# Nine register loads for two, ScalarE scaling B rows in the prologue, and a later conversion of the capacity

## The chip, the cores and the metric

The kernel runs on one core of a Trainium2 chip. The metric is the device time of one execution in microseconds (us); lower is better. One core has five engines that run their own instruction streams in order and wait for each other on semaphores: TensorE (PE, with its weight loads shown apart as PEld), VectorE (DVE), ScalarE (ACT), GpSimd (POOL) and SyncE (SP, which here issues transfers).

## The reference, cut to what matters

Three parts follow one another: a linear attention with a decaying state, an MLP with h·cos(h), and a top-1 mixture of experts.

```python
# attention, chunk by chunk, for each of 4 x 8 heads (768 tokens, head_dim 32, d_state 16)
L = np.exp(cum[..., :, None] - cum[..., None, :]) * causal
y_intra = np.einsum('bhij,bhjd->bhid', np.einsum('bhin,bhjn->bhij', Cc, Bc) * L, xc)
y_inter = np.einsum('bhin,bhnd->bhid', Cc, state) * np.exp(cum)[..., None]
state = decay_full * state + np.sum(Bc * xc * np.exp(cum[..., -1:] - cum), axis=j)
# MLP over 3072 tokens of 256: w_in 256x2048, w_out 2048x256
h = x @ w_in;  x = (h * np.cos(h)) @ w_out
# experts: 8 of them, 256 -> 1024 -> 256, at most `capacity` tokens each
e = argmax(x @ w_gate);  keep the first `capacity` tokens of each expert
out[i] = gate_w[i] * (np.maximum(x[i] @ w1[e], 0) @ w2[e])   # kept tokens only
```

## The kernel before, in words

**Order of the work.** Each piece of work is a Python function that issues its instructions on whatever engines it uses. Pieces are registered with `put(name, fn, args)`; the n-th call for a name takes the n-th slot number of `PLACE[name]`, and at the end all pieces are run sorted by slot (L1739 on). That one order, written out by hand as a table of numbers, is the program order on every engine at once. A prologue that is listed in Python runs ahead of it.

**Attention** (first 300 us or so, mixed with the MLP). Tokens are cut into 24 chunks of 128, two chunks c = 0, 1 to a group g, so 12 groups. For group 1 in the prologue: `a_bcp` broadcasts the running sum of log a into PSUM (`bcp`, L700), `a_expp` turns it on ScalarE into the decay matrix `ex` (L708), `a_mask0` zeroes its upper triangle on GpSimd (L713; all columns but the last), `a_sd` makes the scores `spd` on TensorE (L732), which VectorE multiplies into `ex` (`a_md`, L740). `a_bp` (L676) scales the B rows of a chunk (`xb`, 128 tokens x 8 heads x 16) by the last column of that decay matrix, one factor per token and head; `a_up` and `a_st` (L766, L780 to L784) then build the state, `a_y` (L801, L806) the output, which is turned into `xT` (L845 on ScalarE, L851 on VectorE). The scores of chunk 1 of group 1 go into the PSUM banks in which its `bcp` stood.

**MLP.** Six tiles of 512 tokens. For each of 16 steps: `hp` (L921), on ScalarE and VectorE g = h·cos(h) (L928, L932, L935, L938), then `yt` (L959, L964). Its weights arrive as `pre` or `wst` and are split into a high and a low part by VectorE integer operations (L873, L878, L883).

**Experts.** Tokens are sorted into 29 to 31 blocks of 128 of one expert each, gathered by indirect transfer (L1535, `xr`) and transposed by DMA (L1552, `xkeep`, `xk`). A block has two halves of the hidden layer, so there are 58 jobs: `b_mm1` (L1603, `hp`), ReLU and its low part (L1609 ACT, L1613 DVE, `hr`), the transpose (L1630 `tp` on TensorE, copied by ACT L1639, or by DMA later), `b_mm2` (L1650, `yp`), the scaled sum (L1662, L1664, `yacc`) and the indirect write (L1669). The weights `w1a`, `w1b`, `w2a`, `w2b` of all 8 experts lie in SBUF, and a job picks its expert's by a register of TensorE's sequencer: `w[:, bass.ds(ev[i], 1)]`. The expert numbers of the blocks are worked out on VectorE into `eblk[0]` (blocks 0 to 11) and `eblk[1]` (19 entries from block 12 on; L1143), and `experts(k)` (L1589 to L1594) loads all of one of them with one `reg_load`. The second halves of the weights are still being normed while the first jobs run: `wst` is loaded (L1223), ScalarE sums squares (L1231), TensorE adds these up over partitions (L1235, `pn`), VectorE and others scale (L1240 to L1256).

**Capacity.** It comes as an int64, and `constants2` (slot 100) ends with four tiny VectorE operations that turn it into a float (L456 to L459, `capf`); its first reader is far behind, in the routing of the first tile.

Of the kernel before, what the change touches and what calls it, by code (L numbers as in the profile page):

```python
# [106 lines left out]
    'ete': [1446],
    'ets': [1431],
    'ett': [1438],
    'ex': [67, 116, 114, 159, 115, 240, 203, 390, 476, 493, 590, 597, 603, 738, 769, 849, 816,  # L110
        954, 870, 1082],
# [10 lines left out]
    'gat': [148, 230, 350, 466, 585, 713, 838, 944, 1049, 1185],  # L122
    'id': [1513],
    'in0': [1502],
    'in1': [1667],
    'iv0': [1499],
    'iv1': [1756, 1757, 1762],
    'lt': [1592],
    'lte': [1643],
    'lts': [1607],  # L130
    'ltt': [1623],
# [1680 lines left out]
```

## Time and profile before

| what | value |
| --- | --- |
| median of 3 runs | 568.72 us (568.5 to 569.3) |
| the profiled execution: its own time | 568.56 us |
| the profiled execution: its span | 566.8 us |
| TensorE (PE) busy | 528.7 us, 93% of the span |
| VectorE, ScalarE, GpSimd busy | 73%, 67%, 63% |
| chain that ended last, by engine | PE 45%, DVE 25%, ACT 11%, DMA 7%, issue 6% |
| granted TensorE clock, mean | 0.984 |

The span is counted from the first to the last instruction of the profile; the execution's own time is 1.8 us longer. Busy shares are means over stages with different limits: the first 80 us lean on VectorE and ScalarE, the rest for the most part on TensorE. "issue" is idle time for which the profile has no releaser. A timeline row has the start, the time from there to the end of a group of like instructions, and in brackets how long the engine sat idle before it and for whom.

### The profile page before, as it was taken

The numbers are of one execution on the slowest core, as the hardware profiler recorded it, in microseconds if no ns is written. First come the engines' busy times: TensorE is split into PE (matmuls) and PEld (weight loads), VectorE is DVE, ScalarE is ACT, GpSimd is POOL, SyncE is SP. The second block draws the span as 40 slices with busy tenths as digits, with TensorE's granted clock in tenths as the row PEclk, the third lists the DMA queues.
The fourth block names the chain that finished last, engine by engine and source line by source line (L and its number), as shares of the span: only waits on it lengthen the run. The fifth ranks groups of instructions, "written<-read, shape, count | busy, mean of one in ns | idle before, by whom it ended". The sixth has DMA issues, their size and how long they took to land.

```text
span 566.8 us, 10500 instructions
## 1 busy us (share of the span) xinstructions
PE 528.7 (93%) x3188; PEld 387.9 (68%) x3188; DVE 415.7 (73%) x877; ACT 379.2 (67%) x691; POOL 355.6 (63%) x422
## 2 busy tenths in 40 slices
PE   8778999999999999999999998899589999998993
PEld 7455666877878778887888686665357666665672
DVE  6999985669977987688788999989957632332441
ACT  5448998887788688868887887788388633323210
POOL 5775374878668869876955673887546454312454
PEclk9999999999999999999999998999789999999998
DMA  6898533666264365263522331576587688767882
GB/s 227 276 318 323 191 116 128 186 246 220 94 222 132 99 201 177 82 201 116 166 58 76 85 102 38 144 185 174 139 198 204 113 160 162 157 118 131 152 164 63
DMA packets 110645, 89.91 MB, mean 159 GB/s; under 512 B 64542, under 2 KB 99424, under 8 KB 110592
## 3 DMA queue, kind: packets, MB, share of 16 engines
q1 hardware_dynamic: 107808, 82.26, 52.5%
q0 software_dynamic: 2784, 6.97, 4.8%
q8 instruction: 30, 0.49, 0.4%
q14 instruction: 23, 0.19, 0.1%
HBM read 59.50 MB, written 15.54 MB: 132 GB/s over the span
## 4 chain that ended last, share of the span: by engine, by line
PE 45%; DVE 25%; ACT 11%; DMA 7%; issue 6%; POOL 3%; SPq 1%; POOLq 0%; ACTq 0%; DVEq 0%
PE hp L1603 10%; PE hp L921 9%; PE yp L1650 9%; PE yt L959 7%; DVE g L938 4%; DVE g L932 3%; ACT g L935 3%; DMA out_dram<-yacc,scat 2%; PE yt L964 2%; ACT ex L646 2%; ACT g L928 2%; DVE w2a L1256 1%; DVE xs L1037 1%; POOL out_dram L1669 1%; ACT gh L942 1%
## 5 line engine op out<-in xcount | busy, mean ns | idle before, releaser
L921 PE MATMUL hp<-xT,w_in 128*128 128x512 f32 x576 | 153.7, 406 | 4.7 <-DVE g L938 2.5
L921 PEld LDWEIGHTS hp<-xT,w_in 128*128 128x128 f32 x576 | 104.9, 189 | 35.0 <-DVE g L938 8.8
L947 POOL TENSOR_TENSOR gw<-g,gh 128x512 fp32r<-128x512 f32 x72 | 98.8, 1376 | 47.6 <-ACT gh L942 22.8
L959 PE MATMUL yt<-gh,w_o 128*128 128x512 f32 x320 | 88.4, 398 | 0.1
L935 ACT ACTIVATE g<-g,halfpi 128x512 f32<-128x512 f32 x96 | 67.9, 717 | 27.0 <-DVE g L932 26.4
L1650 PEld LDWEIGHTS <-ht 128*128 128x128 f16 x696 | 68.0, 98 | 20.7 <-issue 2.7
L1609 ACT ACTIVATE hr<-hp 128x512 f16<-128x512 f32 x58 | 33.7, 596 | 72.2 <-PE hp L1603 43.1
L938 DVE TENSOR_TENSOR g<-hp,g 128x512 f32<-128x512 f32 x96 | 65.4, 685 | 18.0 <-ACT g L935 17.8
L932 DVE SCALAR_TENSOR_TENSOR g<-g,hp 128x512 f32<-128x512 f32 x96 | 64.4, 679 | 16.9 <-ACT g L928 16.2
L1613 DVE SCALAR_TENSOR_TENSOR hr<-hp,hr 128x512 f16<-128x512 f32 x58 | 39.2, 686 | 40.0 <-ACT hr L1609 35.6
L959 PEld LDWEIGHTS yt<-gh,w_o 128*128 128x128 f32 x320 | 58.3, 188 | 12.7 <-issue 1.0
L928 ACT ACTIVATE g<-hp 128x512 f32<-128x512 f32 x96 | 55.0, 586 | 17.9 <-PE hp L921 15.3
L942 ACT ACTIVATE gh<-g 128x512 fp32r<-128x512 f32 x80 | 48.7, 622 | 11.0 <-DVE g L938 6.5
L959 PE MATMUL yt<-gw,w_o 128*128 128x512 f32 x160 | 50.9, 399 | 1.6 <-POOL gw L947 0.8
L1535 POOL DMA_INDIRECT xr<-xs_d,gat x29 | 34.3, 1181 | 20.0 <-DMA xk<-xr 7.5
L1650 PE MATMUL yp<-w2b,ht 128*128 x348 | 43.2, 272 | 1.7 <-ACT yacc L1662 1.6
L1650 PE MATMUL yp<-w2a,ht 128*128 x348 | 44.2, 274 | 0.4 <-ACT ht L1639 0.4
L1669 POOL DMA_INDIRECT out_dram<-yacc,scat x29 | 28.9, 997 | 23.1 <-DVE yacc L1664 15.7
L629 POOL TENSOR_TENSOR ex<-ex,ncum 128x512 f32<-128x512 f32 x32 | 37.5, 1193 | 3.3 <-DMA ex<-cumc_d 2.1
L1657 POOL TENSOR_TENSOR sc<-gall,invb 128x1 f32<-128x1 f32 x58 | 12.7, 231 | 42.2 <-ACT yacc L1662 30.9
L1664 DVE SCALAR_TENSOR_TENSOR yacc<-yp,sc,yacc 128x256 f32<-128x256 f32 x29 | 13.5, 481 | 32.3 <-PE yp L1650 23.6
L959 PEld LDWEIGHTS yt<-gw,w_o 128*128 128x128 f32 x160 | 29.5, 189 | 11.1 <-POOL gw L947 3.3
(244 smaller groups left out, 995.3 us busy)
## 6 DMA issues: line engine op xcount, KB each, us to landing
wst<-in_w_dram SPq DMA_DIRECT2D x32, 512.0 KB
ex<-cumc_d SPq DMA_DIRECT2D x10, 1024.0 KB
pre<-in_w_io_dram SPq DMA_DIRECT2D x14, 512.0 KB
hl_d<-hl SPq DMA_DIRECT2D x10, 512.0 KB
b<-hl_d SPq DMA_DIRECT2D x10, 512.0 KB
c4s<-hl_d SPq DMA_DIRECT2D x40, 128.0 KB
xb<-in_xB_dram SPq DMA_DIRECT2D x11, 384.0 KB
xs_d<-xs SPq DMA_DIRECT2D x6, 514.0 KB
```

Of the source, the lines that this page charges most:

```text
L629: nc.gpsimd.tensor_tensor(lt, lt, nn, op=ALU.add)
L921: nc.tensor.matmul(hp, w_in[:, f, wl, k, :], xT[:, k, xl, :], start=(n == 0), stop=(n == 5))
L928: nc.scalar.activation(g, HP[it], AF.Copy, bias=MAGIC + 0.25)
L932: nc.vector.scalar_tensor_tensor(g, g, MAGIC, HP[it], op0=ALU.subtract, op1=ALU.subtract)
L935: nc.scalar.activation(GT[it], GT[it], AF.Sin, scale=SIN_SCALE, bias=halfpi)
L938: nc.vector.tensor_tensor(GT[it], HP.pop(it), GT[it], op=ALU.mult)
L942: nc.scalar.activation(h, GT[it], AF.Copy)
L947: eng.tensor_tensor(l, GT.pop(it), GH[it][0].bitcast(F32), op=ALU.subtract)
L959: nc.tensor.matmul(YT[t][k], WO['w'][:, f, o, k * P:(k + 1) * P], r, start=(f == 0 and n == 0), stop=(f == NF - 1 and n == 2))
L1603: nc.tensor.matmul(hp, XK[i][:, 2 * xl + k, :], w[:, bass.ds(ev[i], 1), k, wl, :].rearrange("p a b -> p (a b)"), start=(n == 0), stop=(n = ...
L1613: nc.vector.scalar_tensor_tensor(hr[:, 1], HPB.pop(j), 0.0, hr[:, 0], op0=ALU.max, op1=ALU.subtract)
L1650: nc.tensor.matmul(yp, ht[:, hk, :], w[:, bass.ds(e, 1), k, wl, :].rearrange("p a b -> p (a b)"), start=(k == 0 and n == 0), stop=(k == 3 ...
```

## The change

Three edits, and a renumbering of the table that carries them.

First, `experts` loads a range of blocks and is called nine times, for 3, 3, 3, 3 registers of `eblk[0]` and 3, 3, 4, 4, 5 of `eblk[1]`; the same 31 registers in all. Second, the scaling of group 1's B rows, two VectorE operations in the prologue, becomes 16 ScalarE activations with a per-partition scale, 8 for each chunk. Third, the four capacity operations leave `constants2` and become a piece `cap` at slot 236. The rest of the table is only renumbered: apart from these pieces each engine has the order of before, and the orders of GpSimd and SyncE are the same throughout.

```diff
 PLACE = {
+    'cap': [236],
-    'ex0': [1472],
-    'ex1': [1658],
...
+    def cap_float():
         ci = cap_i.bitcast(I32)
         t = mp.tile([P, 4], F32, name="capt")
         nc.vector.tensor_copy(t[:, 0:2], ci)
...
+    def a_bpa(g, c):
+
+        d = G[g]
+        d['bp'] = d['btok']
+        bp = d['btok'][:, c, :].rearrange("p (v n u) -> p v n u", v=2, u=4)
+        for h in range(H):
+            x = bp[:, h // 4, :, h % 4]
+            nc.scalar.activation(x, x, AF.Copy, scale=d['lt'][c][:, h, P - 1:P])
...
-        (a_bp, 1, 0, V),
+        (a_bpa, 1, 0),
...
-        (a_bp, 1, 1, V),
+        (a_bpa, 1, 1),
...
-    def experts(k):
-        lo, hi = LOS[k]
-        regs = [nc.tensor.alloc_register(f"e{i}") for i in range(lo, hi)]
-        nc.tensor.reg_load(regs, eblk[k][0:1, 0:hi - lo])
-        for i, r in zip(range(lo, hi), regs):
+    def experts(k, a, b):
+        regs = [nc.tensor.alloc_register(f"e{i}") for i in range(a, b)]
+        nc.tensor.reg_load(regs, eblk[k][0:1, a - LOS[k][0]:b - LOS[k][0]])
+        for i, r in zip(range(a, b), regs):
             ev[i] = nc.tensor.snap(r, min_val=0, max_val=E - 1)
...
-    put('ex0', experts, 0)
+    for a, b in ((0, 3), (3, 6), (6, 9), (9, NE)):
+        put(f'e{a}', experts, 0, a, b)
...
-    put('ex1', experts, 1)
+    for a, b in ((12, 15), (15, 18), (18, 22), (22, 26), (26, LOS[1][1])):
+        put(f'e{a}', experts, 1, a, b)
```

On TensorE the second load of before (19 registers) stands between a job's `yp` and the next job's `hp`; the rows are those of before, where ISA is a register operation of the sequencer.

```order
L1650 LDWEIGHTS ht
L1650 ISA
L1650 MATMUL yp_4562<-w2a,ht 128x256
L1603 LDWEIGHTS xkeep_4156
L1592 TENSOR_LOAD eblk_90
L1594 ISA x2
L1603 ISA
L1603 MATMUL hp_4621<-w1a,xkeep_4156 128x512
```

In the changed kernel the same place has no load:

```order
L1668 LDWEIGHTS ht
L1668 ISA
L1668 MATMUL yp_4579<-w2a,ht 128x256
L1621 LDWEIGHTS xkeep_4166
L1621 ISA
L1621 MATMUL hp_4599<-w1a,xkeep_4166 128x512
```

One of the five that stand for it, the load of 4 registers for blocks 22 to 25, comes 930 rows further on, again between two `hp`:

```order
L1621 ISA
L1621 MATMUL hp_5189<-w1b,xk 128x512
L1621 LDWEIGHTS xk
L1610 TENSOR_LOAD eblk_90
L1612 ISA
L1621 MATMUL hp_5208<-w1a,xk 128x512
```

So one long load has become five short ones, each just ahead of the first job that needs it. On ScalarE in the prologue, before (`bcp_234` and `bcp_233` are the two PSUM banks of group 1's chunk 1):

```order
L651 ACTIVATE ex<-ex 128x256
L708 ACTIVATE ex<-bcp_234,ncum 128x128 x4
L892 ACTIVATE w_in<-w1a 128x256
L708 ACTIVATE ex<-bcp_233,ncum 128x128 x4
L845 ACTIVATE xT<-yp 128x2x128 x2
```

and in the changed kernel:

```order
L660 ACTIVATE ex<-ex 128x256
L696 ACTIVATE xb<-xb,ex 128x16 x8
L726 ACTIVATE ex<-bcp_234,ncum 128x128 x4
L910 ACTIVATE w_in<-w1a 128x256
L726 ACTIVATE ex<-bcp_233,ncum 128x128 x4
L696 ACTIVATE xb<-xb,ex 128x16 x8
L863 ACTIVATE xT<-yp 128x2x128 x2
```

The first eight scalings have moved in ahead of the two banks' exponentials, the second eight behind them. On VectorE the four capacity operations, in the changed kernel, stand between a weight split and the h·cos(h) step that followed it before:

```order
L773 TENSOR_TENSOR ex<-sp,ex 128x2x2x128
L901 SCALAR_TENSOR_TENSOR w1a<-pre,w1a 128x512
L465 CAST capt<-cap_i 128x2
L466 TENSOR_SCALAR capt<-capt 128x1
L467 TENSOR_TENSOR capt<-capt 128x1
L468 SCALAR_TENSOR_TENSOR capf<-capt 128x1
L950 SCALAR_TENSOR_TENSOR g<-g,hp 128x512
```

Before, these four stood in the prologue behind a state update (L784) and ahead of a weight split (L873), and here L883 was followed by L932 at once.

## Rows read from the trace of the kernel before

**Rows 1.** The timeline of PE, 414 to 430: start, us, line, [idle before].

```profile
418.67 2.72 PE L1603 MATMUL hp<-w1a,xkeep 128*128 x6 [2.21 <-issue]
421.18 1.05 PE L1630 MATMUL tp<-ncum,hr 128*128 128x128 f16 x8
...
427.91 0.28 PE L1235 MATMUL pn<-wsc,ones_f 128*128 128x2 f32 x2
```

**Rows 2.** Stretches: us; busy PE, PEld, DVE, ACT, POOL; clock, DMA, GB/s.

```profile
419.00:422.00 3.00, 3.00 (x14) 1.55 (x13) 0.33 (x2) 1.06 (x4) 1.38 (x3) 0.50 0.64 180
...
470.00:500.00 30.00, 30.00 (x205) 19.88 (x204) 9.54 (x17) 10.20 (x20) 12.32 (x26) 1.00 0.83 160
```

**Rows 3.** Tile eblk: ns least/median/most, first to last start (us).

```profile
L1592 PEldq TENSOR_LOAD <-eblk x2: 1165/1507/1849, 365.8 to 416.1; - x2
...
L1736 PEldq TENSOR_LOAD <-eblk x1: 312/312/312, 475.3 to 475.3; - x1
```

**Rows 4.** The timeline of DVE, 415 to 419.

```profile
417.75 0.69 DVE L1613 SCALAR_TENSOR_TENSOR hr<-hp,hr 128x512 f16<-128x512 f32 x1
```

**Rows 5.** The timeline of ACT, 416 to 429.

```profile
424.19 1.14 ACT L1250 ACTIVATE w2b<-wst,wsc 128x1024 f16<-128x1024 f32 x1
425.23 1.04 ACT L1231 ACTIVATE w2b<-wst 128x1024 f16<-128x1024 f32 x1
...
426.27 1.04 ACT L1231 ACTIVATE w2b<-wst 128x1024 f16<-128x1024 f32 x1
427.21 0.19 ACT L1231 ACTIVATION_READ_ACCUMULATOR w2b<-wst 128x1 f32 x1
```

**Rows 6.** The stretch of a DMA burst, columns as in rows 2.

```profile
423.20:425.50 2.30, 2.30 (x20) 1.45 (x19) 1.48 (x2) 1.77 (x4) 2.08 (x2) 1.00 0.92 280
```

**Rows 7.** Line 1603 between 462.85 and 463.65.

```profile
L1603 PEldq FUSED_REGOPS  x6: 51/55/55, 462.9 to 463.6; - x6
...
L1603 PE MATMUL hp<-w1a,xk x1: 379/379/379, 463.6 to 463.6; 128*128 x1
```

**Rows 8.** The timeline of DVE in the prologue, 20 to 37.

```profile
20.82 2.28 DVE L676 TENSOR_TENSOR xb<-xb,ex 128x128 f32<-128x128 f32 x2
23.03 1.87 DVE L740 TENSOR_TENSOR ex<-spd,ex 128x512 f32<-128x512 f32 x3
...
31.09 0.15 DVE L456 CAST capt<-cap_i 128x2 f32<-128x2 int32 x1
...
31.74 0.42 DVE L873 TENSOR_SCALAR w1a<-pre 128x512 int32<-128x512 int32 x1
...
33.34 1.23 DVE L883 SCALAR_TENSOR_TENSOR w1a<-pre,w1a 128x512 int32<-128x512 int32 x1
```

**Rows 9.** The timeline of ACT in the prologue.

```profile
18.52 1.18 ACT L708 ACTIVATE ex<-bcp,ncum 128x128 f32<-128x128 f32 x4
...
32.57 0.38 ACT L845 ACTIVATE xT<-yp 128x256 fp32r<-128x256 f32 x1 [1.45 <-PE yp L806]
```

**Rows 10.** The chain of waits, 30 to 92: start, us, what.

```profile
71.70 1.16 ACT ex L636 x4
```

**Rows 11.** The timeline of PE in the prologue.

```profile
19.84 1.10 PE L732 MATMUL spd<-pre,bc 128*128 128x512 f32 x2
...
21.44 1.13 PE L732 MATMUL spd<-pre,x 128*128 128x512 f32 x2
```

**Rows 12.** The timeline of POOL in the prologue.

```profile
32.97 1.04 POOL L629 TENSOR_TENSOR ex<-ex,ncum 128x512 f32<-128x512 f32 x1 [2.09 <-DMA ex<-cumc_d]
```

**Rows 13.** The timelines of DVE and ACT, 61 to 65.

```profile
62.73 0.67 DVE L932 SCALAR_TENSOR_TENSOR g<-g,hp 128x512 f32<-128x512 f32 x1
...
63.44 0.72 ACT L935 ACTIVATE g<-g,halfpi 128x512 f32<-128x512 f32 x1
```

**Rows 14.** Busy time by stretch, columns as in rows 2.

```profile
66.00:72.00 6.00, 6.00 (x24) 3.76 (x23) 6.00 (x11) 5.97 (x9) 3.78 (x3) 1.00 0.85 302
```

**Rows 15.** The timeline of all engines, 73.8 to 79.

```profile
77.16 1.22 PEld L921 LDWEIGHTS hp<-xT,w_in 128*128 128x128 f32 x6 [0.30 <-DVE g L938]
```

More of the change, by code (lines that the diff above doesn't have):

```diff
@@ L23 @@
 PLACE = {
[5 rows of a table removed]
-    'ass': [505, 593, 714, 827, 940, 1068, 1188, 1292],
[51 rows of a table removed]
-    'chi': [401, 430, 436, 485, 442, 510, 500, 536, 535, 553, 571, 579, 608, 626, 630, 635, 647,
[7 rows of a table removed]
-    'clo': [407, 456, 455, 494, 477, 524, 521, 541, 538, 567, 572, 595, 615, 627, 640, 652, 660,
[6 rows of a table removed]
-    'con': [100],
-    'cp': [188, 327, 352, 483, 628, 726, 836, 965, 1093, 1224],
-    'css': [1523, 1570, 1609, 1639, 1670, 1687, 1709, 1747],
[5 rows of a table removed]
-    'dfi': [206, 212, 232, 236, 345, 285, 302, 328],
-    'et': [1404],
-    'et2': [1427],
@@ L107 @@
[L107 to L111, printed above, removed]
-    'ex0': [1472],
-    'ex1': [1658],
-    'exp': [163, 256, 347, 451, 586, 719, 829, 942, 1064, 1199],
-    'frc': [131, 143, 173, 191, 200, 207, 229, 243, 262, 283, 292, 317, 310, 321, 360, 366, 396,
[6 rows of a table removed]
[L122 to L131, printed above, removed]
[20 rows of a table removed]
-    'mul': [139, 152, 179, 199, 208, 222, 248, 257, 276, 294, 308, 330, 354, 335, 367, 377, 400,
[6 rows of a table removed]
[5 rows of a table added]
+    'ass': [506, 594, 715, 828, 941, 1069, 1189, 1293],
[49 rows of a table added]
+    'cap': [236],
+    'cd': [1488, 1541, 1576, 1623, 1636, 1668, 1676, 1723],
+    'ch': [1548, 1578, 1620, 1649, 1680, 1697, 1721, 1767],
+    'chi': [402, 431, 437, 486, 443, 511, 501, 537, 536, 554, 572, 580, 609, 627, 631, 636, 648,
[7 rows of a table added]
@@ new lines @@
+    'clo': [408, 457, 456, 495, 478, 525, 522, 542, 539, 568, 573, 596, 616, 628, 641, 653, 661,
[6 rows of a table added]
+    'con': [100],
+    'cp': [188, 328, 353, 484, 629, 727, 837, 966, 1094, 1225],
+    'css': [1525, 1573, 1613, 1643, 1674, 1692, 1714, 1752],
[5 rows of a table added]
+    'dfi': [206, 212, 232, 237, 346, 286, 303, 329],
+    'e0': [1473],
+    'e12': [1673],
+    'e15': [1691],
+    'e18': [1761],
+    'e22': [1811],
+    'e26': [1877],
+    'e3': [1507],
+    'e6': [1553],
+    'e9': [1612],
+    'et': [1405],
+    'et2': [1428],
@@ new lines @@
+    'ete': [1447],
+    'ets': [1432],
+    'ett': [1439],
+    'ex': [67, 116, 114, 159, 115, 241, 203, 391, 477, 494, 591, 598, 604, 739, 770, 850, 817,
+        955, 871, 1083],
+    'exp': [163, 257, 348, 452, 587, 720, 830, 943, 1065, 1200],
+    'frc': [131, 143, 173, 191, 200, 207, 229, 244, 263, 284, 293, 318, 311, 322, 361, 367, 397,
[6 rows of a table added]
+    'gat': [148, 230, 351, 467, 586, 714, 839, 945, 1050, 1186],
+    'id': [1515],
+    'in0': [1503],
+    'in1': [1670],
+    'iv0': [1500],
+    'iv1': [1762, 1763, 1768],
@@ L159 @@
+    'lt': [1595],
+    'lte': [1647],
+    'lts': [1610],
+    'ltt': [1627],
[20 rows of a table added]
+    'mul': [139, 152, 179, 199, 208, 222, 249, 258, 277, 295, 309, 331, 355, 336, 368, 378, 401,
[6 rows of a table added]
     'p0': [0],
@@ L256 @@
     'p99': [118],
-    'raw': [65, 275, 353, 468, 599, 717, 822, 945, 1048],
[4 rows of a table removed]
-    'rev': [402, 403, 658, 661, 889, 895, 1113, 1123, 1328, 1329, 1517, 1520],
-    'rex': [1245, 1405, 1576],
-    'rg1': [565, 783, 1016, 1232, 1359, 1567],
-    'rg2': [625, 846, 1083, 1295, 1421, 1578],
-    'rh0': [479, 689, 957, 1192, 1370, 1535],
-    'rh2': [502, 775, 984, 1280, 1385, 1557],
-    'rl0': [497, 745, 967, 1195, 1384, 1545],
-    'rl2': [648, 847, 1039, 1299, 1397, 1581],
-    'rnd': [130, 137, 158, 181, 180, 197, 223, 242, 246, 278, 277, 315, 304, 319, 349, 351, 379,
[10 rows of a table removed]
@@ L281 @@
-    'rst': [662, 923, 1122, 1300, 1434, 1599],
-    'rx0': [406, 675, 901, 1127, 1332, 1521],
-    'rx1': [432, 670, 912, 1132, 1330, 1522],
-    'rx2': [471, 712, 953, 1167, 1352, 1540],
-    'rx3': [450, 706, 917, 1139, 1334, 1537],
-    's0': [169, 218, 269, 306, 358, 382, 487, 480, 589, 606, 728, 786, 869, 893, 995, 974, 1107,
-        1088, 1225, 1235],
-    's1': [171, 201, 279, 272, 365, 370, 518, 515, 598, 644, 737, 765, 879, 884, 1007, 1021,
-        1087, 1098, 1207, 1209],
-    'sin': [135, 149, 174, 194, 205, 217, 244, 254, 268, 287, 300, 322, 323, 324, 361, 374, 397,
[6 rows of a table removed]
@@ L297 @@
-    'sml': [87],
-    'sph': [58, 93, 288, 371, 491, 650, 789, 845, 998, 1063],
-    'spi': [109, 160, 348, 423, 556, 707, 797, 891, 1030, 1133],
-    'spl': [69, 102, 301, 394, 537, 665, 796, 872, 1026, 1121],
-    'st': [220, 299, 337, 368, 411, 452, 580, 624, 715, 724, 766, 819, 915, 960, 1031, 1054,
-        1102, 1196, 1243, 1479],
-    'u': [183, 291, 329, 340, 380, 434, 526, 558, 699, 703, 735, 807, 890, 909, 993, 1042, 1094,
-        1190, 1222, 1419],
-    'ud': [1276, 1349, 1400, 1455],
@@ L306 @@
-    'uh': [1325, 1371, 1435, 1506],
-    'ul': [1344, 1351, 1408, 1409, 1476, 1463, 1515, 1530],
-    'un': [1287, 1360, 1411, 1461],
-    'used': [1863],
-    'uss': [1312, 1369, 1429, 1486],
[7 rows of a table removed]
-    'wih': [64, 136, 166, 161, 182, 190, 214, 215, 251, 281, 271, 289, 293, 309],
-    'wil': [70, 147, 170, 168, 189, 209, 231, 216, 253, 297, 273, 311, 331, 333],
-    'wld': [113, 103, 127, 108, 140, 86, 162, 219, 195, 224, 196, 245],
-    'woh': [312, 320, 336, 373, 356, 341, 392, 409, 413, 425, 375, 459, 506, 503, 447, 539],
@@ L322 @@
-    'wol': [313, 334, 343, 386, 378, 381, 393, 435, 443, 446, 453, 484, 520, 507, 522, 614],
-    'x': [125, 226, 305, 420, 562, 638, 778, 833, 990, 1180],
-    'yg': [250, 344, 438, 583, 716, 806, 932, 1043, 1147, 1265],
-    'zero': [499],
+    'raw': [65, 276, 354, 469, 600, 718, 823, 946, 1049],
[4 rows of a table added]
+    'rev': [403, 404, 659, 662, 890, 896, 1114, 1124, 1329, 1330, 1519, 1522],
+    'rex': [1246, 1406, 1579],
+    'rg1': [566, 784, 1017, 1233, 1360, 1570],
+    'rg2': [626, 847, 1084, 1296, 1422, 1581],
@@ new lines @@
+    'rh0': [480, 690, 958, 1193, 1371, 1537],
+    'rh2': [503, 776, 985, 1281, 1386, 1560],
+    'rl0': [498, 746, 968, 1196, 1385, 1547],
+    'rl2': [649, 848, 1040, 1300, 1398, 1584],
+    'rnd': [130, 137, 158, 181, 180, 197, 223, 243, 247, 279, 278, 316, 305, 320, 350, 352, 380,
[10 rows of a table added]
+    'rst': [663, 924, 1123, 1301, 1435, 1602],
+    'rx0': [407, 676, 902, 1128, 1333, 1523],
+    'rx1': [433, 671, 913, 1133, 1331, 1524],
+    'rx2': [472, 713, 954, 1168, 1353, 1542],
+    'rx3': [451, 707, 918, 1140, 1335, 1539],
@@ new lines @@
+    's0': [169, 218, 270, 307, 359, 383, 488, 481, 590, 607, 729, 787, 870, 894, 996, 975, 1108,
+        1089, 1226, 1236],
+    's1': [171, 201, 280, 273, 366, 371, 519, 516, 599, 645, 738, 766, 880, 885, 1008, 1022,
+        1088, 1099, 1208, 1210],
+    'sin': [135, 149, 174, 194, 205, 217, 245, 255, 269, 288, 301, 323, 324, 325, 362, 375, 398,
[6 rows of a table added]
+    'sml': [87],
+    'sph': [58, 93, 289, 372, 492, 651, 790, 846, 999, 1064],
+    'spi': [109, 160, 349, 424, 557, 708, 798, 892, 1031, 1134],
+    'spl': [69, 102, 302, 395, 538, 666, 797, 873, 1027, 1122],
@@ new lines @@
+    'st': [220, 300, 338, 369, 412, 453, 581, 625, 716, 725, 767, 820, 916, 961, 1032, 1055,
+        1103, 1197, 1244, 1480],
+    'u': [183, 292, 330, 341, 381, 435, 527, 559, 700, 704, 736, 808, 891, 910, 994, 1043, 1095,
+        1191, 1223, 1420],
+    'ud': [1277, 1350, 1401, 1456],
+    'uh': [1326, 1372, 1436, 1508],
+    'ul': [1345, 1352, 1409, 1410, 1477, 1464, 1517, 1532],
+    'un': [1288, 1361, 1412, 1462],
+    'used': [1870],
+    'uss': [1313, 1370, 1430, 1487],
[7 rows of a table added]
+    'wih': [64, 136, 166, 161, 182, 190, 214, 215, 252, 282, 272, 290, 294, 310],
@@ L326 @@
+    'wil': [70, 147, 170, 168, 189, 209, 231, 216, 254, 298, 274, 312, 332, 334],
+    'wld': [113, 103, 127, 108, 140, 86, 162, 219, 195, 224, 196, 246],
+    'woh': [313, 321, 337, 374, 357, 342, 393, 410, 414, 426, 376, 460, 507, 504, 448, 540],
+    'wol': [314, 335, 344, 387, 379, 382, 394, 436, 444, 447, 454, 485, 521, 508, 523, 615],
+    'x': [125, 226, 306, 421, 563, 639, 779, 834, 991, 1181],
+    'yg': [251, 345, 439, 584, 717, 807, 933, 1044, 1148, 1266],
+    'zero': [500],
 }
@@ L1419, in fused_kernel @@
     put('con', constants2)
+    put('cap', cap_float)
     for g in range(2, NG):
```

262 rows, old and new, of the table PLACE are left out of this document.

## The prediction

> **What bounds the kernel now.** I read three views, in the order in which a saved microsecond would have to travel. First, the stretches: from 470 to 500 TensorE is busy for 30.00 of 30.00 us at the full clock [rows 2], and the stretches beside it look alike; so the end of the kernel is TensorE's own stream, and what TensorE loses ahead of it is lost for good, while what other engines save counts only if TensorE was waiting for them. Second, the timeline of TensorE around 416, where the change takes a load away: it sat idle for 2.21 us ahead of `hp`, with no releaser [rows 1]. The view of the tile `eblk` names it: a register load of 1849 ns that starts at 416.1 on TensorE's sequencer [rows 3]. Third, the prologue and the 40 us behind it. There VectorE and ScalarE have next to no idle time (6.00 and 5.97 of 6.00 us from 66 to 72, [rows 14]), and at 77.16 TensorE's weight loads have waited for VectorE's L938 [rows 15]: in this part a VectorE operation on the chain does cost.
>
> **The change, part by part: the loads.** What the load of 19 registers costs TensorE: 2.21 us of idle time, and then an `hp` of 2.72 us [rows 1] in a stretch whose granted clock is 0.50 [rows 2], the lower of the two levels; at the full clock it takes half of that, 1.36 less. The transpose behind it is slowed too. Together some 3.6 us. The other load of before (12 registers, 1165 ns at 365.8) held up nothing, as I read TensorE's timeline there: its sequencer was far ahead.
>
> What comes back of it? Without the load, `hp` starts at about 416.4 and ends at 417.8. Next is `tp`, which needs VectorE's L1613. That starts at 417.75 and takes 0.69 [rows 4], so `tp` can't start before some 418.5. It started at 421.18 [rows 1]: at most 2.7 us are gained here. Then comes the norm of the weights. The `pn` at 427.91 [rows 1] adds up what ScalarE's L1231 has summed, and that pair began at 425.23 and 426.27, its last sum read by 427.4 [rows 5]. The second of the two needs a `wst` that lands with the burst of 423.2 to 425.5 [rows 6]; its transfers were issued by SyncE at 419.3 and 419.9, as the timeline of that queue shows, behind a gather and not behind TensorE. So the second L1231 can't begin before 425.5, and `pn` not before 425.5 + 1.04 + 0.19 + 0.05 = 426.8. TensorE, which could be there at 425.2, waits. Gain: 427.9 − 426.8 = **1.1 us**. Behind it I find no wait of TensorE's that isn't itself driven by TensorE, so it should last to the end. Ends: 0.7 (the sums start no earlier than that pair's order on ScalarE allows) and 2.7 (the weights bind nothing).
>
> What the nine short loads cost: 1165 ns for 12 and 1849 for 19 registers [rows 3] make 97 ns for each and nothing fixed; three, four and five are 0.29, 0.39 and 0.49 us. Behind the old load it took 0.7 us from its end (416.1 + 1.85 = 418.0) to the matmul at 418.67; with fewer registers I take 0.3. So a short load wants 0.6 to 0.8 us by which the sequencer must run ahead. That lead can be read: ahead of the place of the load for blocks 22 to 25 the register operations begin at 462.9 and their first matmul at 463.6, a lead of 0.7 [rows 7]. It is the shortest; in the same view the other new places that matter give 0.9, 0.9, 1.0, 1.3, 1.8 and 2.2. Cost: nothing to 0.1 us, and I take **0**. The upper bound is the row of one register, 312 ns [rows 3]: with 97 for each further one, four take 0.6, and with the 0.3 behind them 0.2 us are short at the one place. These numbers stand against a rule of the Trainium skill. The Trainium skill ("Runtime: NRT & Kernel Launch", "Instruction fetch mechanics") gives about 200 ns per register even in bulk. This trace has 97, from SBUF; by the page's figure (an estimate: 0.6, 0.8, 1.0 us and the 0.3) the stalls over the leads would add up to some 0.6 us.
>
> **The scalings.** VectorE loses two operations of 2.28 us together at 20.82, behind which three products L740 stood at 23.03 [rows 8]. But ScalarE gets eight activations ahead of the exponentials of the first bank, which end at 18.52 + 1.18 = 19.70 [rows 9]; and the `spd` that is written into that bank starts at 19.84 [rows 11], right behind them. What is one of them worth? Four L636, 128 elements with a pointer operand, are 1.16 us on the chain, 0.29 each [rows 10]; L1250 with 1024 elements and a pointer leaves ScalarE after 425.23 − 424.19 = 1.04 [rows 5]. The slope is 0.75 / 896 = 0.84 ns, so 16 elements take 0.29 − 112 × 0.84 ns = 0.20 us, and eight take 1.6. TensorE's `spd` at 19.84 moves to 21.4, and with it the `spd` at 21.44 to 23.0, done at 24.15 instead of 22.57. That is the operand of the third L740, which ran at 24.2 in before (23.03 + 2 × 0.6). So VectorE does the first two products early, then idles until 24.2: **0** gained. Ends: at 0.10 per scaling, as for L1231 and its read together less the elements (1.04 − 0.86 = 0.19 for two, [rows 5]), it is 0.8 us early; at 0.29 it is 0.7 late. Lateness is absorbed: L883 at 33.34 took 1.23 [rows 8] beside GpSimd's L629, which starts at 32.97 behind a DMA [rows 12], some 0.6 more than its like elsewhere. The second eight scalings end near 24.4, far ahead of their matmul.
>
> **The capacity.** The four operations took 31.09 to 31.74, 0.65 us [rows 8]. Taking them out there buys nothing: what follows ends in an L851 at 33.0 that needs ScalarE's L845, done at 32.57 + 0.38 = 32.95 [rows 9], and that comes from a state update ahead of the four. In the new place they stand ahead of L932 at 62.73, and ScalarE's L935 follows at 63.44 [rows 13], 0.04 behind the end of L932 and with nothing else to do for 0.15. From there both engines are full up to TensorE's wait at 77.16. So 0.65 us late go through: **+0.6**. If something between them has slack, 0.
>
> **The sum.** 568.56 (the profiled execution's own time; the median is 568.72) − 1.1 + 0 + 0 + 0.6 = 568.06, so **568.1**. 0.2%, or 1.1 us, is about what a measurement of this kernel can tell from no change.
>
> **The rivals.**
> (A) The weights do not bind: all of 2.7 comes back at 416. For it: `tp` could run at 418.5. Against it: the DMA burst. 568.56 − 2.7 + 0.6 = 566.5, faster.
> (B) The capacity is hidden in 62 to 77: 568.56 − 1.1 = 567.5, at the edge. For it: 15 us of mixed engines; against it: both are full.
> (C) The scalings cost 0.10 each: VectorE is 0.8 early at 24 and reaches L883 ahead of GpSimd's L629, which pays for the capacity: 567.4, faster.
> (D) Slower: a load has a fixed price, however few registers. For it: a load of one register took 504, 808 and 1126 ns on other engines in the same view of `eblk`, and two rows are a thin base for a slope. At 1.2 us each, with the 0.3 behind it, the five leads of 0.7 to 1.3 are short by 0.8 + 0.6 + 0.6 + 0.5 + 0.2 = 2.7: 570.8. It decides from about 1.0 us per load. Against it: 312 ns on TensorE itself.
> (E) A price per register of twice the slope, and stalls of 0.6: 568.7, the same. The page of the Trainium skill named above would have it so. The rows speak against it.
>
> **Chances.** Forecast 0.42, its own range 567.2 to 568.9; A 0.17; B 0.16; C 0.09; D 0.09; E 0.07. Faster by over 0.2%: A, C, two thirds of B, and a little of the forecast: 0.39. Slower: D and a little: 0.11. Within 0.2%: 0.50. The range reaches to A below, 565.9, and takes in a stalled load above, 569.5; outside are most of D and the far end of A.
>
> **What would show it.** Right: no idle time ahead of `hp` near 416.5 and a full clock from 417 to 422; `tp` near 418.5; TensorE waiting for ScalarE ahead of the second `pn`; register loads of 0.3 to 0.5 us with no idle time on TensorE; the third L740 (a line 18 further on) at 24.2, with VectorE idle ahead of it; TensorE waiting 0.6 longer near 77. Wrong: a `pn` that doesn't wait (A); an L883 ahead of L629 in the prologue (C); idle time ahead of the matmul behind a short load (D, E); or the 1.1 us given back to a wait after 430 that I took for TensorE's own.

## The result, and the profile after

The changed kernel is slower: 572.44 us in the median of 11 runs (570.6 to 574.8), against 567.98 for the kernel before on the same chip (11 runs). The ratio is 1.008, with a 95% interval of 1.0061 to 1.0100. The forecast was 568.1 us, no measurable change, with a range that ended at 569.5. The profiled execution took 571.37 us, 2.8 more than that of before, with a mean granted clock of 0.981 (0.984 before).

Where the time went is read from three views. First the tile `eblk`, as in [rows 3]: each row has the instruction, how many, its least, median and most ns, and its first and last start.

```profile
L1610 PEldq TENSOR_LOAD <-eblk x9: 766/1054/1960, 366.4 to 481.1; - x9
...
L1756 PEldq TENSOR_LOAD <-eblk x1: 382/382/382, 478.1 to 478.1; - x1
```

No load of three to five registers took less than 766 ns, though 12 registers took 1165 before and 19 took 1849. In order, the nine took 1.30, 0.78, 1.05, 0.77, 0.79, 0.77 (three registers each), 1.79, 1.61 (four) and 1.96 us (five).

The timeline of TensorE (start, us, and in brackets the idle time before), around the old load's place, which answers to [rows 1], and then behind the last three new loads:

```profile
417.99 1.46 PE L1621 MATMUL hp<-w1a,xkeep 128*128 x6
419.28 0.61 PE L1648 MATMUL tp<-ncum,hr 128*128 128x128 f16 x8
420.99 0.38 PE L1253 MATMUL pn<-wsc,ones_f 128*128 128x2 f32 x2 [1.10 <-ACT w2b L1249]
...
424.49 0.61 PE L1648 MATMUL tp<-ncum,hr 128*128 128x128 f16 x8 [0.31 <-issue]
...
427.54 0.32 PE L1253 MATMUL pn<-wsc,ones_f 128*128 128x2 f32 x2
...
447.90 1.74 PE L1668 MATMUL yp<-w2a,ht 128*128 x12 [0.99 <-ACT w2b L1268]
...
466.55 1.46 PE L1621 MATMUL hp<-w1a,xk 128*128 x6 [1.23 <-issue]
...
483.37 1.81 PE L1668 MATMUL yp<-w2a,ht 128*128 x12 [0.93 <-issue]
```

The stretches beside [rows 2], columns as there:

```profile
419.00:422.00 3.00, 1.90 (x20) 1.45 (x18) 2.66 (x9) 3.00 (x7) 1.47 (x3) 1.00 0.56 144
...
470.00:500.00 30.00, 29.07 (x201) 19.31 (x200) 9.55 (x16) 8.34 (x17) 11.73 (x25) 1.00 0.76 142
```

The gain is there as forecast: `hp` follows at once, runs at the full clock and takes half of its 2.72 us; `tp` starts at 419.28 for 421.18. So are new holes, 0.99, 1.23 and 0.93 us, in a stretch in which TensorE had none; each begins while its sequencer is in one of the late loads. The first of them shows how a releaser can mislead: it names ScalarE's L1268, but in the experiments below that replace this load by a cheap one the same matmul doesn't wait. Set side by side, a matmul of after stands 1.7 us later than the same one of before at 413, 0.4 earlier at the second `pn` (427.54 for 427.91), 1.2 later at 448, 2.9 at 467, 4.5 at 482, and 3.9 when TensorE ends. The span grew by less, 2.8, since what follows TensorE's end took 1.1 less.

In the prologue, the timelines of TensorE, VectorE and ScalarE, which answer to [rows 8, 9, 11] (L758 is the L740 of before, L750 its L732):

```profile
20.81 1.10 PE L750 MATMUL spd<-pre,bc 128*128 128x512 f32 x2 [1.81 <-POOL bc L678]
...
22.41 1.12 PE L750 MATMUL spd<-pre,x 128*128 128x512 f32 x2
...
20.07 1.27 DVE L758 TENSOR_TENSOR ex<-spd,ex 128x512 f32<-128x512 f32 x2
23.57 0.69 DVE L758 TENSOR_TENSOR ex<-spd,ex 128x512 f32<-128x512 f32 x1 [2.23 <-PE spd L750]
...
17.78 1.85 ACT L696 ACTIVATE xb<-xb,ex 128x16 f32<-128x16 f32 x8
```

ScalarE's first eight scalings take 1.85 us, both pairs of `spd` start 1.0 later than before (19.84 and 21.44 there), and VectorE sits idle for 2.23 us ahead of the third product.

And in the first tile, the timelines that answer to [rows 13, 15]:

```profile
62.25 0.16 DVE L465 CAST capt<-cap_i 128x2 f32<-128x2 int32 x1
...
62.90 0.68 DVE L950 SCALAR_TENSOR_TENSOR g<-g,hp 128x512 f32<-128x512 f32 x1
...
63.61 0.72 ACT L953 ACTIVATE g<-g,halfpi 128x512 f32<-128x512 f32 x1 [0.70 <-DVE g L950]
...
77.50 1.23 PEld L939 LDWEIGHTS hp<-xT,w_in 128*128 128x128 f32 x6 [0.30 <-DVE g L956]
```

The capacity operations now stand ahead of L950, and the weight loads that wait for VectorE start at 77.50, for 77.16 before.

### The profile page after: what moved, and what is told of

It is laid out like the page before. It is cut to its first block, busy times and chain, and to the rows that moved or that the text cites. A ratio compares the mean times of both kernels' runs of the same rounds, so it can differ in the third digit from the quotient of the medians.

```text
span 569.6 us, 10523 instructions
## 1 busy us (share of the span) xinstructions
PE 531.1 (93%) x3188; PEld 388.0 (68%) x3188; DVE 414.9 (73%) x875; ACT 382.2 (67%) x707; POOL 355.3 (62%) x422
## 5 line engine op out<-in xcount | busy, mean ns | idle before, releaser
L950 DVE SCALAR_TENSOR_TENSOR g<-g,hp 128x512 f32<-128x512 f32 x96 | 64.5, 678 | 17.2 <-ACT g L946 16.7
L1668 PE MATMUL yp<-w2a,ht 128*128 x348 | 46.0, 277 | 2.5 <-ACT w2b L1268 1.0
L638 POOL TENSOR_TENSOR ex<-ex,ncum 128x512 f32<-128x512 f32 x32 | 37.6, 1197 | 3.6 <-PE up L784 2.4
```

The source lines that it names most:

```text
L638: nc.gpsimd.tensor_tensor(lt, lt, nn, op=ALU.add)
L950: nc.vector.scalar_tensor_tensor(g, g, MAGIC, HP[it], op0=ALU.subtract, op1=ALU.subtract)
L1668: nc.tensor.matmul(yp, ht[:, hk, :], w[:, bass.ds(e, 1), k, wl, :].rearrange("p a b -> p (a b)"), start=(k == 0 and n == 0), stop=(k == 3 ...
```

## The experiments

Unless it says otherwise each was timed in five rounds (12 runs) beside the kernel before on the same chip; brackets hold the 95% interval of the ratio.

**1. The nine loads alone** (`e1_loads_only`): the changed `experts` and its nine calls; scaling and capacity as before.

> The kernel before with the nine register loads alone; the scaling and the capacity stay as before. Theory L (the whole loss comes from the loads: each holds TensorE's sequencer for 0.8 to 2.0 us whatever its number of registers, five of them stall TensorE behind 423): 1.006 to 1.010 of before, idle time of about 1 us ahead of the matmul behind each of the loads of 4, 4 and 5 registers. Rival P (the prologue edits carry a good part of the loss, through the 0.65 us of the capacity in the first tile): loads alone within 0.3% of before.

Measured: 571.01 us against 567.7, ratio 1.0058 [1.0037, 1.0079]. Its tile `eblk`, and its timeline of TensorE at the two `pn` and behind the last three loads:

```profile
L1598 PEldq TENSOR_LOAD <-eblk x9: 774/1242/2237, 365.1 to 480.5; - x9
...
418.71 0.38 PE L1242 MATMUL pn<-wsc,ones_f 128*128 128x2 f32 x2 [0.84 <-ACT w2b L1238]
...
426.65 0.38 PE L1242 MATMUL pn<-wsc,ones_f 128*128 128x2 f32 x2 [1.16 <-ACT w2b L1238]
...
447.37 1.74 PE L1656 MATMUL yp<-w2a,ht 128*128 x12 [1.01 <-ACT w2b L1257]
...
466.01 1.46 PE L1609 MATMUL hp<-w1a,xk 128*128 x6 [1.22 <-issue]
...
483.10 1.81 PE L1656 MATMUL yp<-w2a,ht 128*128 x12 [1.20 <-issue]
```

The loads alone make most of the loss. The return at 416 is as forecast, down to the wait of the second `pn` for the weights, 1.26 us earlier than before (0.9 counted from 413, where this trace was 0.4 ahead already); from there to 482 the trace loses 5.4 us, 3.55 of it in four holes right behind loads (0.12, 1.01, 1.22, 1.20).

**2. The scaling alone** (`e2_scale_only`): `a_bpa` for `a_bp`, the rest as before.

> The kernel before with the 16 ScalarE scalings alone. Theory L, from the comparison of the two traces (TensorE 0.5 us earlier from 46 on): 0.5 us less than before, 0.999, if it lasts to the end. Rival P: 0 or more, as the score that follows the first eight scalings is late by 1 us.

Measured: 567.83 against 567.7, ratio 0.9996 [0.9973, 1.0020]. In its timelines the second pair of `spd` starts at 22.37; in experiment 1, whose prologue is that of before, at 20.70, so it moved by 1.67 us (1.6 by the forecast). The interval takes in both values that were expected, 0.999 and 1.000. The third product stands where it stood, with VectorE idle ahead of it:

```profile
22.37 1.12 PE L741 MATMUL spd<-pre,x 128*128 128x512 f32 x2
...
23.54 0.69 DVE L749 TENSOR_TENSOR ex<-spd,ex 128x512 f32<-128x512 f32 x1 [2.19 <-PE spd L741]
```

(The profile of before itself lost 0.75 us at 16 that experiments 1 to 3 did not lose, so prologues are compared with experiment 1.)

**3. The capacity alone** (`e3_cap_only`): `cap_float` as a piece in the first tile.

> The kernel before with the capacity's four operations moved to the first tile alone. My forecast of record and rival P: 0.6 us more, 1.001. If something between 62 and 77 has slack: 0, 1.000.

Measured: 567.55 against 567.7, ratio 1.0007 [0.9989, 1.0025]. The weight loads that wait for VectorE, in experiment 1 and, second, here:

```profile
76.34 1.23 PEld L928 LDWEIGHTS hp<-xT,w_in 128*128 128x128 f32 x6 [0.30 <-DVE g L945]
```

```profile
77.10 1.23 PEld L923 LDWEIGHTS hp<-xT,w_in 128*128 128x128 f32 x6 [0.30 <-DVE g L940]
```

0.76 us later there, for 0.65 put in. That is too little for the medians, whose interval takes in both 1.000 and 1.001.

**4. Other counts at the same places** (`e4_swap`): the first twelve in one load, the rest as 4, 5, 3, 3, 4 where the change has 3, 3, 4, 4, 5.

```diff
-    put('ex1', experts, 1)
+    put('e12', experts, 1, 12, 16)
+    put('e16', experts, 1, 16, 21)
+    put('e21', experts, 1, 21, 24)
+    put('e24', experts, 1, 24, 27)
+    put('e27', experts, 1, 27, LOS[1][1])
```

> The kernel before with the first load whole (12 registers) and the second split into 4, 5, 3, 3 and 4 registers at the five places of the changed kernel, where these held 3, 3, 4, 4 and 5. Theory N (the number of registers in a load decides: up to three 0.77 to 1.05 us, four and five 1.6 to 2.0): the loads at 423 and 430 take 1.6 to 2.0, those at 446 and 465 take 0.8. Rival T (the place decides, by the transfers that run then): 0.8 at 423 and 430, 1.6 to 1.8 at 446 and 465, as in the changed kernel. Time: N 1.004 to 1.008, T 1.006 to 1.010.

Measured: 569.54 against 567.7, ratio 1.0021 [1.0003, 1.0038]. The five took 0.79, 0.81, 1.37, 0.92 and 1.67 us, with holes of 0.27, 0, 0.57, 0.52 and 0.62. Five registers (0.81) were cheaper than three (1.37): the price is neither one per register nor one per load. Neither expectation came true: the loads at 423 and 430 were cheap, against N, and the time is below what both had. (The profiled run, 572.72, was the slowest of the twelve.)

**5. Other starts** (`e5_offsets`, one run): the two loads of before, and six (`experts2`, a copy of `experts`) that load again numbers which TensorE already has. Both rows of numbers begin at a 16-byte boundary, and a number has 4 bytes.

```diff
+    put('x0', experts2, 1, 24, 28)   # slot 1669.7
+    put('x1', experts2, 1, 18, 22)   # 1686.7
+    put('x2', experts2, 1, 12, 16)   # 1755.7
+    put('x3', experts2, 0, 0, 4)     # 1804.7
+    put('x4', experts2, 0, 4, 8)     # 1869.7
+    put('x5', experts2, 0, 8, 11)    # 1920.7
```

> The kernel before with six extra loads of registers that are loaded already, in this order: from eblk[1] four registers at its bytes 48 to 63 (near 423) and at 24 to 39 (near 430), then four at bytes 0 to 15 of it (near 446), and from eblk[0] four at 0 to 15 (near 465), four at 16 to 31 (near 481), three at 32 to 43 (near 495). Theory T (the place in the run decides): the first two take 0.8 us, the next three 1.4 to 1.8, as the loads there did before. Rival O (the address within eblk decides, since the slow loads of the two kernels were all from bytes 24 on of eblk[1]): the first two take 1.6 to 1.8, the third to fifth 0.8. Rival N (the number of registers): all of four alike.

Measured: 569.28 in one run (567.27 before). The six, then the two old ones:

```profile
L1601 PEldq TENSOR_LOAD <-eblk x6: 332/342/1182, 422.7 to 499.0; - x6
L1591 PEldq TENSOR_LOAD <-eblk x2: 1347/1706/2066, 365.7 to 416.6; - x2
```

In order 0.35, 1.18, 0.34, 0.34, 0.33 and 1.12 us: the four loads of four numbers that begin at a 16-byte boundary cost a third of a microsecond and left no hole; the same count from 8 bytes past one, and three from a boundary, cost over three times that. None of the three expectations had this.

**6. One register at a time** (`e6_singles`): the nineteen as nineteen loads, each right ahead of its block's first job.

```diff
-    put('ex1', experts, 1)
+    put('e12', experts, 1, 12, 13)
+    put('e13', experts, 1, 13, 14)
...
+    put('e30', experts, 1, 30, 31)
```

> The kernel before with the first load whole and the second replaced by a load of one register ahead of the first job of each block from 12 on, the last two of the 19 behind all other jobs. A load of one register took 0.31 to 0.43 us on TensorE at 475 to 482 in six traces. Theory S (that holds everywhere, and with the 0.2 behind it lies below the lead of 0.7 to 1.0): no idle time at the loads, and the 1.1 us of the removed load are kept: 0.998. Rival (even a single load takes 0.8 in places, or the leads are used up): 0.1 to 0.3 us idle at several of 17 places, 1.001 to 1.005.

Measured: 570.03 against 567.27, ratio 1.0051 [1.0026, 1.0077]. Its tile `eblk` (the twenty hold the load of twelve too), and one of the holes:

```profile
L1609 PEldq TENSOR_LOAD <-eblk x20: 297/309/1352, 367.0 to 550.1; - x20
...
492.65 1.45 PE L1620 MATMUL hp<-w1b,xk 128*128 x6 [0.38 <-issue]
```

Even loads of one register are not always hidden. At seven places where an `hp` follows a `yp` loads of 0.30 to 0.62 us left holes of 0.04 to 0.40, four of them 0.36 to 0.40. The ratio is at the upper end of what the rival had.

**7. The long load where TensorE waits anyway** (`e7_at_pn`): the kernel before, with its 19 registers loaded ahead of the first `pn`.

```diff
-    'ex1': [1658],
+    'ex1': [1661.5],
```

> The kernel before with its load of 19 registers moved past one hp and one tp, to stand right ahead of the first pn, for which TensorE waits 1.1 us in the changed kernel and in the loads alone. If that wait is ScalarE's and DMA's and not TensorE's, about 1 us of the 2.2 is hidden: 0.998, the second half of the norms arriving as before. If the wait moves with TensorE, no change: 1.000.

Measured: 566.47 (564.6 to 568.1) against 567.27, ratio 0.9989 [0.9965, 1.0014]. TensorE's timeline:

```profile
417.66 0.61 PE L1630 MATMUL tp<-ncum,hr 128*128 128x128 f16 x8
419.95 0.35 PE L1235 MATMUL pn<-wsc,ones_f 128*128 128x2 f32 x2 [1.68 <-ACT hr L1609]
...
426.10 0.28 PE L1235 MATMUL pn<-wsc,ones_f 128*128 128x2 f32 x2
```

and VectorE's, for the account below:

```profile
417.82 0.68 DVE L1613 SCALAR_TENSOR_TENSOR hr<-hp,hr 128x512 f16<-128x512 f32 x1
```

The load of 2.14 us is hidden in part here: TensorE is idle for 1.68 us ahead of the first `pn`, where it waits 0.84 and 0.80 for ScalarE in experiments 1 and 11, which have no load there. In this trace TensorE stands 1.8 us earlier than before from 424 to 467 and 2.8 at its end; the medians show 0.8 of that, and don't tell it from nothing.

**8. The change without its nine loads** (`e8_two_loads`): scaling and capacity, and the two loads of before.

> The changed kernel with the two loads of before: scaling on ScalarE and capacity in the first tile together. If the edits add up (0.9996 and 1.0007 by themselves): 1.000, and the changed kernel's 1.008 is the loads' 1.006 and noise. If the two together cost what neither does alone: 1.002 or more.

Measured: 568.51 against 567.27, ratio 1.0018 [0.9993, 1.0043]; with experiment 1 that is 1.0076 of the change's 1.0080. The interval takes in 1.000 and 1.002, so whether the two edits cost anything is not shown.

**9. Fours from a boundary** (`e9_fours`): twelve in one load, then 4, 4, 4, 4 and 3 at the change's five places.

```diff
-    put('ex1', experts, 1)
+    put('e12', experts, 1, 12, 16)
+    put('e16', experts, 1, 16, 20)
+    put('e20', experts, 1, 20, 24)
+    put('e24', experts, 1, 24, 28)
+    put('e28', experts, 1, 28, LOS[1][1])
```

> The kernel before with the first load whole and the second split into 4, 4, 4, 4 and 3 registers, each load from a 16-byte boundary on, at the five places of the changed kernel. Theory A (a load from a 16-byte boundary of up to four registers is one access and takes 0.33 to 0.36 us, one that crosses a boundary or is odd in size takes several and 0.8 to 2.2; in the run with extra loads five of six such loads of four took 0.33 to 0.36): four loads of 0.35, the last 0.8 to 1.1, no idle time ahead of them but 0 to 0.3 at the last, and the gain of the removed load is kept: 0.997 to 0.999 of before. Rival (the first touch of fresh values is slow, or the wait ahead of the first: the load of four from a boundary took 0.79 when it was the first of its tile): 0.8 or more at each, up to 0.3 us idle at several, 1.000 to 1.003.

Measured: 570.86 against 570.22, ratio 1.0012 [0.9989, 1.0036]. The fours took 0.35, 0.58, 0.33 and 0.33 us and left no hole, the three 1.38 us and a hole of 0.32. The loads are near what was expected, the time is not: 0.997 to 0.999 had been expected, and the interval takes in only the end of that.

**10. Other sizes** (`e10_sizes`, one run): seven more loads of numbers already loaded; 4 and 2 from a boundary, then five times 3, from 8, 12, 8 and 4 bytes past one and from one.

> The kernel before with seven extra loads of registers that are loaded already, at new places and sizes: four at a 16-byte boundary of eblk[1] (near 423), two at a boundary of eblk[0] (near 430), three of eblk[1] at 8 bytes past one (near 444), three of eblk[0] at 12 past (446), three of it at 8 past (465), three at 4 past (481), three of eblk[1] at a boundary (495). Theory A: 0.35, 0.35, and 0.7 to 1.4 for each of the threes. Rival N2 (a load of up to four registers that have been read before is 0.35 whatever its address, as a fresh value costs more): 0.35 for all seven, against which the run before had 1.18 and 1.12 for two of them.

Measured: 575.94 in one run (570.22 before); in order 0.35, 0.55, 0.77, 1.13, 1.04, 1.43 and 1.45 us. The two took 0.55 where 0.35 had been expected. A three is dear from any start, and the later ones were dearer than the first.

**11. The last load filled up to four** (`e11_fours_padded`): as experiment 9, but the last load also takes the row's twentieth entry, which no job uses.

```diff
-    put('e28', experts, 1, 28, LOS[1][1])
+    put('e28', experts, 1, 28, 32)
```

> Loads alone; no scaling and no capacity. The first twelve registers in one load as before; the other nineteen as five loads of four, each from a 16-byte boundary, at the five places of the change; the last of them takes one entry more than it needs (the twentieth, which no job uses). Theory (a load of four from a 16-byte boundary takes about 0.35 us anywhere, and what else a load asks for is more): all five take 0.33 to 0.6 us, the last too, which took 1.38 with three registers; no idle time above 0.2 us on TensorE behind any of them, the second pn waits for ScalarE, and about 1.1 us are left at the end: ratio 0.998, within 0.996 to 1.000. Rival 1 (a late place makes a load dear, whatever it asks for): the last load takes 1.0 us or more and leaves 0.3 us or more idle; ratio 1.001 as with the unpadded five. Rival 2 (the stall is no matter of the load's duration): idle time behind loads of 0.35 us.

Measured: 566.69 against 567.79, ratio 0.9995 [0.9979, 1.0011]. Its tile `eblk` (the six hold the load of twelve, 1312), and TensorE:

```profile
L1595 PEldq TENSOR_LOAD <-eblk x6: 333/340/1312, 365.7 to 476.9; - x6
...
425.42 0.38 PE L1239 MATMUL pn<-wsc,ones_f 128*128 128x2 f32 x2
...
465.80 1.78 PE L1653 MATMUL yp<-w2a,ht 128*128 x12 [0.35 <-DMA ht<-hr]
```

All five took 0.33 to 0.35 us without a hole behind any; one register more made the last load four times cheaper (1.38 to 0.34). The second `pn` didn't wait and stood 2.5 us earlier than before. Of these 1.1 were left at the end: some 0.8 went where TensorE ran into a transpose by DMA (`ht` above) that had not been late before, some 0.6 around 480, where the timeline names no wait.

**12. The change with its loads mended** (`e12_change_padded`): scaling, capacity, and the loads of experiment 11.

> The whole change, with its nine loads replaced by one of twelve and five of four from 16-byte boundaries, the last with one unused entry more. Theory (the loads' stalls are what the change costs, the scaling is worth nothing, the capacity 0.6 us): 1.1 less and 0.6 more than before, ratio 0.999, within 0.997 to 1.001; against 1.008 for the change as made. Rival (some other part of the change costs, or the three together): 1.003 or more.

Measured: 567.15 (565.9 to 568.2) against 567.79, ratio 0.9991 [0.9973, 1.0009]. The tile `eblk`, and TensorE's longest hole behind a load:

```profile
L1607 PEldq TENSOR_LOAD <-eblk x6: 332/444/1062, 367.2 to 478.6; - x6
...
423.69 0.61 PE L1645 MATMUL tp<-ncum,hr 128*128 128x128 f16 x8 [0.49 <-issue]
```

The loads took 1.06 (twelve), 1.01, 0.55, 0.34, 0.33 and 0.33 us, with a hole of 0.49 behind the 1.01 and one of 0.09 behind the first 0.33. With other loads and nothing else altered the change is 5 us faster than as it was made.

**13. Reads, registers or places** (`e13_reads`, one run): seven more loads, which test a model of the loads seen till then. By it a load reads four neighbours from a 16-byte boundary at once and each other number by itself.

```diff
+    put('x0', experts2, 0, 4, 12)    # 8 from a boundary, slot 1669.7
+    put('x1', experts2, 0, 4, 11)    # 7, 1686.7
+    put('x2', experts2, 1, 12, 28)   # 16, 1745.7
+    put('x3', experts2, 1, 12, 27)   # 15, 1755.7
+    put('x4', experts2, 1, 16, 24)   # 8, 1804.7
+    put('x5', experts2, 1, 16, 23)   # 7, 1869.7
+    put('x6', experts2, 1, 18, 26)   # 8, 8 bytes past, 1920.7
```

> The two loads of before, and seven further loads of numbers that TensorE has already, at seven places behind block 14's: 8 registers from a 16-byte boundary, 7 from a boundary, 16 from a boundary, 15 from a boundary, again 8 and 7 from a boundary, and 8 that begin 8 bytes past one. Theory (a load reads four neighbours from a 16-byte boundary at once and every other register by itself, and each such read costs 0.25 to 0.48 us): reads 2, 4, 4, 6, 2, 4 and 5, so 0.5 to 1.0 us, 1.0 to 1.9, 1.0 to 1.9, 1.5 to 2.9, 0.5 to 1.0, 1.0 to 1.9 and 1.25 to 2.4; above all, seven registers take longer than eight at both pairs of places, and fifteen longer than sixteen. Rival 1 (a price per register, with or without a fixed part): eight take longer than seven and sixteen longer than fifteen, and the start of the eight doesn't matter. Rival 2 (the place in the program sets the price): the loads grow dearer along the list whatever they ask for, the second eight dearer than the first seven. With seven more loads the time is above that of before in any case.

Measured: 574.63 in one run (569.81 before). The tile `eblk`, asked for one load at a time, in that order:

```profile
L1603 PEldq TENSOR_LOAD <-eblk x1: 1010/1010/1010, 422.9 to 422.9; - x1
L1603 PEldq TENSOR_LOAD <-eblk x1: 1058/1058/1058, 429.8 to 429.8; - x1
L1603 PEldq TENSOR_LOAD <-eblk x1: 1114/1114/1114, 443.0 to 443.0; - x1
L1603 PEldq TENSOR_LOAD <-eblk x1: 2510/2510/2510, 446.2 to 446.2; - x1
L1603 PEldq TENSOR_LOAD <-eblk x1: 605/605/605, 466.0 to 466.0; - x1
L1603 PEldq TENSOR_LOAD <-eblk x1: 1702/1702/1702, 481.6 to 481.6; - x1
L1603 PEldq TENSOR_LOAD <-eblk x1: 3279/3279/3279, 501.8 to 501.8; - x1
```

Fifteen took 2.51 us and sixteen 1.11; seven took 1.70 and eight 0.61 (1.06 and 1.01 at the first pair, which tells nothing); eight from another start took five times the eight from a boundary. Neither the number of registers nor the place gives this; the number of reads gives the order within each pair. The last load, 3.28, is above the 2.4 that I had allowed five reads.

## Why the prediction was wrong

**The step that failed** is "three, four and five are 0.29, 0.39 and 0.49 us", and with it "Cost: nothing to 0.1 us, and I take 0". A slope was laid through two rows [rows 3] that differ in more than their registers. Counted in reads, the 12 are three and the 19 seven (four fours and three single ones): 0.39 and 0.26 us per read. The nine loads are 31 reads, where the two of before are 10 and the mended six are 8:

| load | reads | us, all runs |
| --- | --- | --- |
| 1 register | 1 | 0.30 to 0.68 (median 0.31 in experiment 6) |
| 4 from a boundary | 1 | 0.33 to 0.35 in 16 of 20, else 0.55 to 1.01 |
| 2 | 2 | 0.55 |
| 5 from a boundary | 2 | 0.81 |
| 8 from a boundary | 2 | 0.61, 1.01 |
| 3 | 3 | 0.77 to 1.45 (21 loads) |
| 12 | 3 | 1.06 to 1.36 |
| 4 from elsewhere | 4 | 1.18 to 1.81 (6 loads) |
| 16; 7 from a boundary | 4 | 1.11; 1.06, 1.70 |
| 5, 8 from 8 bytes past one | 5 | 1.96, 2.24; 3.28 |
| 15; 19 | 6; 7 | 2.51; 1.85 to 2.16 |

The row of one register, 312 ns, was among the rows and is about the price of a read; it had been taken as a bound from which further registers cost 97 ns. The Trainium skill ("Runtime: NRT & Kernel Launch", "Instruction fetch mechanics") puts loads of registers, which it describes as coming from HBM, at about 200 ns per register. The loads from SBUF here have 70 ns per register (16 at once) to 480 (a three of 1.45 us), and 300 to 680 for a single one: no price per register fits them, neither that of the Trainium skill nor mine.

**The leads were right.** In the changed kernel's trace a load less its hole is 0.5, 0.8, 0.4 and 1.0 us at the four places with a hole behind 420; with the 0.3 allowed behind a load that is a lead of 0.8, 1.1, 0.7 and 1.3, and 0.7 to 1.3 had been read from the trace of before. (What was said of the change was not exact: not every load stands just ahead of the first job that needs it. Those for blocks 22 and 26 on stand two and three `hp` ahead of it. The leads were read where the loads stand.) Only the loads that have to fit into them were 2.6 to 4.6 times longer than planned.

**Rival D** had the direction, the place of the holes and nearly the time (570.8), and was given 0.09. Its mechanism, a fixed price per load, is wrong: a four costs less than a three. Rival E had such stalls too, but at 0.6 us in all. C did not happen: the changed kernel's L883 (there L901) started at 32.60, not ahead of GpSimd's L629 (there L638, 32.51). A's sign is there, since the second `pn` of the changed kernel's own trace didn't wait (427.54, above), but TensorE came to it late, 1.7 us behind before at 413; A's time, 566.5, is far off.

**The return at 416** came as forecast in the loads-alone trace (1.26 for 1.1, `pn` at 426.65 for "not before 426.8"). The bound is softer than the prediction has it: in experiments 7 and 11 the second `pn` ran at 426.10 and 425.42 without a wait. The transfers that it needs were issued at 417.9 and 417.0 there, at 418.8 in experiment 1 and at 419.3 before, so their time was not as fixed as had been taken. Another bound was misread: "`tp` can't start before some 418.5". In experiment 7 `tp` ran at 417.66, ahead of VectorE's L1613 at 417.82, so that is not the operation it needs; as `pn` comes later, nothing in the sum hangs on it.

**The scalings** are worth nothing that can be measured, by the forecast's own chain: 0.2 us each, `spd` 1.67 later, the third product unmoved. (One of the two ends had a slip, 1.04 − 0.86 is 0.18 and not 0.19; nothing hangs on it.)

**The capacity** costs 0.6 to 0.8 us at TensorE's wait, as forecast ("0.65 us late go through"); that it lasts to the end is not shown. In their traces the whole change is behind its loads alone by 1.0 us at 71, by 2.1 at 413, by 0.9 at the second `pn`, where the earlier of the two had to wait, and ahead by 0.25 at the end: what is late there is absorbed by such waits. The median of experiment 3 allows 0 as well as 0.6.

**Put together.** Ratio 1.0058 for the loads, 1.0018 for the other two; with the loads mended 0.9991, which is what the sum of the prediction says for loads that cost nothing (568.06 / 568.56). That it fits to the last digit is luck: the intervals are about 1 us to either side, and experiments 8 and 11 multiplied give 1.0013. Of the 5.4 us that the loads-alone trace loses behind 427, the holes are 3.55. Behind two of the holes of the changed kernel's trace the `yp` group takes 1.74 and 1.81 us for 1.47, at a granted clock of 1.00. In experiment 11 a `yp` behind an idle time for a transfer takes 1.78 as well, so the slower group seems to go with the idle time, whatever made it; that is argued, not tried. What stays open is why a read costs 0.26 us in one load of three and 0.48 in another (0.66 in the last load of experiment 13; the late ones are dearer on the whole), and why four of the twenty aligned fours, all at the first two places, were not cheap.

No version beats the kernel before by more than can be measured; experiments 7, 11 and 12 (0.9989 to 0.9995 of before) beat the changed one (1.008) by 0.9%, some 5 us.

## What to carry to other kernels

A slope through two rows is a guess about what the rows have in common; before a long operation is cut into pieces, the nearest row of a piece (here one register, 312 ns) is the price to plan with, and registers times that price the first estimate (0.94 us for three, which took 0.77 to 1.45). Here a load of registers wants to begin at a 16-byte boundary and to be filled up to four (experiment 11), or to stand where its engine waits anyway (experiment 7). In both the medians can't be told from those of the kernel before, while three registers in a full stretch cost up to a microsecond. Where a row names a releaser ahead of an idle time, look whether the engine's own sequencer was busy through it.

## What the runs showed of the hardware that had not been expected

- A register load from SBUF was cheap in whole fours from a 16-byte boundary and dear otherwise: 8 numbers from a 16-byte boundary took 0.61 us and 7 took 1.70; 16 took 1.11 and 15 took 2.51; 8 from 8 bytes past a boundary took 3.28.
- With TensorE full, its sequencer ran 0.7 to 1.3 us ahead at the four late places that left a hole, but less at some `hp` behind a `yp`: in experiment 6 four loads of 0.31 to 0.62 us left holes of 0.36 to 0.40 there.
